# A sliding-window attention, Fourier and two-matrix kernel on one core: half of W1's casts on VectorE, fewer filler matmuls, batch 1 and a transform's column steps placed closer

## The chip, the core and the metric

The kernel runs on one core of a Trainium2 chip. The metric is the device time of one execution, in microseconds (us); the median of several runs stands for a kernel. An engine runs its own instructions in the order in which the program lists them for it, so an instruction that waits holds up all behind it on that engine.

## The reference, cut to what matters

```
# q, k, v: 8 batches, 8 heads, 576 positions, 64 wide; window 128
scores = q @ k.T / 8 + slope[h] * -(i - j)     # where 0 <= i-j < 128, else -1e9
attn   = exp(scores - max) / (sum + 1e-9)
x      = attn @ v                              # laid out as (8, 576, 512)
X      = real(fft(fft(x, axis=1), axis=2))
u      = x + X
un     = (u - mean(u)) / sqrt(var(u) + 1e-6)
out    = u + max(un @ w_ch1, 0) @ w_ch2        # 512 x 2048, 2048 x 512
```

## The kernel before, in words

The program is one list of steps, each put into a queue with a time in units of its own (a step of 1 is some five microseconds on the chip). The queue is emptied in order of these times, which is the program's order; a scheduler then fixes each engine's order from it. Who moves a step's time so moves instructions on the engines.

**Attention** works on pairs of heads; there are four pairs in each of eight batches, numbered 0 to 31. Pair `p` of batch `b` begins at `BEGIN[b] + 6 * PACE[b] * j`. `scores` (L403) multiplies queries and keys, three groups of tiles per pair and two heads each (`sp0`, `sp1`). The two heads use the upper and the lower 64 rows of the array. VectorE adds the distance bias (L417), ScalarE takes the exponential (L163 of ScalarE), TensorE turns the result (`turn`, L444), ScalarE copies it out (`pt`, L447), TensorE multiplies by the values (`values`, L461, one accumulator `pv` in one bank), and VectorE divides into the batch's tile `X` (`weigh`, L482 to L486). Batches 0 and 1 do this in f32; later batches split numbers into f16 pairs.

**The weights** W1 and W2 come as 16 chunks each (`weights`). A chunk is loaded (L196) into one of four buffers for W1 and three for W2, so chunk c waits until chunk c-4 or c-3 has been used. `rebias` (L205) casts a 16-bit half of it into a staging tile, `join` (L210, VectorE) puts the halves together, and `gram` (L218, four matmuls) adds to a sum of squares. After the sixteenth chunk a total (L148) gives one scale; then `high` (L236, ScalarE) and `low` (L239, VectorE) make the f16 pair of each of eight groups.

**The Fourier transform of batch 0** (`fourier`, b = 0) is a chain written as a list of steps, `CHAIN` = 0.15 apart: three times fold (L532 to L553, VectorE) and row matmuls (L589), with 24 matmuls on zeros (L602) behind the first two; copies out (L608); the middle (L614); column matmuls (L641) for three blocks, each with `cols_out` (L652 to L656, ScalarE) and `cols_add` (L662 to L676, VectorE); then statistics (L687), the root (L693, L694 on GpSimd), the normalised rows `un` (L702), their turn on TensorE (L711) and the split into f16 (L716, L717). With that done the first feed-forward matmuls (L816, later L830) can start. These use the scaled W1, then W2. The other seven batches have a looser chain (f16, L582, L644).

`busy` issues `SPIN` = 2 matmuls of 512 columns on a constant (L310) behind each group of scores of pairs 0 to 3; their result is never read.

VectorE's instructions of the first 25 steps are tied behind batch 0's chain: where a step of the chain was put, later VectorE work stays behind it.

Of the kernel before, what the change touches and what calls it, by code (L numbers as in the profile page):

```python
# [12 lines left out]
BF16 = mybir.dt.bfloat16  # L13
I32 = mybir.dt.int32
I16 = mybir.dt.int16
AF = mybir.ActivationFunctionType
# [30 lines left out]

LB, LC = 2, 5
DFT = 24 + LC + 0.4
PACE = (0.37, 0.7, 0.85, 0.9, 0.95, 1.0, 1.0, 1.0)  # L50
CHAIN = 0.15
STRETCH = (0.5, 0.7, 1.0, 1.15, 1.25, 1.25, 1.25, 1.25)
BEGIN = (0.0, 9.2, 26.0, 46.4, 68.0, 90.8, 114.8, 138.8)
FORWARD = (22, 41.6, 64.7, 88.7, 112.7, 136.7, 160.7, 184.7, 208.7)
SPIN = 2


def begin_of(p):
    b, j = divmod(p, 4)
    return BEGIN[b] + 6 * PACE[b] * j  # L60


def transform_of(b):
    return BEGIN[b] + PACE[b] * DFT

# [10 lines left out]
def attn_fft_ffn_kernel(  # L76
# [17 lines left out]
    V, A, G, T = nc.vector, nc.scalar, nc.gpsimd, nc.tensor  # L94
# [12 lines left out]
    rel_sb = const.tile([128, 1152], BF16, name="rel_sb")  # L107
# [38 lines left out]
    def total(m):  # L146
        sums = ps_d.tile([128, 512], F32, name="pd")[:, 0:m.shape[1]]
        T.matmul(sums, misc[:, 7:8].broadcast_to([128, 128]), m, start=True, stop=True)  # L148
        return sums

    def root_inv(dst, src):
        V.tensor_scalar(dst, src, 0.5, 2.0 ** -81, ALU.mult, ALU.max)  # L152
        V.tensor_scalar(dst.bitcast(I32), dst.bitcast(I32), 1, 0x3F800000, ALU.logical_shift_right, ALU.bitwise_and)
        V.reciprocal(dst, dst)
# [4 lines left out]
    def put(t, f, *a, **kw):  # L159
        heappush(queue, (t, next(order), lambda *a: f(*a, **kw), a))  # L160
# [12 lines left out]
    def place(b, t, f, *a, **kw):  # L173
        if b == 0:
            put(t, lambda: link(f, *a, **kw))
        else:
            put(t, lambda: f(*a, **kw))
# [5 lines left out]
    def weights(wi, t0, dt, t1, dt1):  # L183
        w, top = ((w1, 2.0 ** 7), (w2, 2.0 ** 14))[wi]
        raws, box = {}, {}
        if wi == 0:
            stages = [hbuf[:, o:o + 1024] for o in range(0, 4096, 1024)]
        else:
            third = dft.tile([128, 2, 4, 256], F16, name="uT", bufs=3).rearrange("p e c t -> p (e c t)").bitcast(F32)
            stages = [stage[:, 0:1024], stage[:, 1024:2048], third]  # L190
        ns = len(stages)

        def load(c):
            raws[c] = stages[c % ns]
            behind[0] = c if wi == 0 else -15 if c < ns else None
            nc.sync.dma_start(out=raws[c].bitcast(I16)[:, 0:2047],  # L196
                              in_=w[:, c * 512:(c + 1) * 512].bitcast(I16)[:, 1:2048])

        def words(c):
            return (wall[1][:, 0, c % 2 * 512:c % 2 * 512 + 512],  # L200
                    wall[wi][:, 1 + c // 2, c % 2 * 512:c % 2 * 512 + 512])

        def rebias(c):
            upper = words(c)[0].bitcast(F16).rearrange("p (x e) -> p x e", e=2)[:, :, 1]
            A.activation(upper, raws[c].bitcast(BF16).rearrange("p (x e) -> p x e", e=4)[:, :, 2], AF.Copy)  # L205

        def join(c):
            upper, dst = (x.bitcast(I32) for x in words(c))
            lower = raws[c].bitcast(I32).rearrange("p (x e) -> p x e", e=2)[:, :, 0]
            V.scalar_tensor_tensor(dst, lower, 13, upper, ALU.logical_shift_right, ALU.bitwise_or)  # L210

        def gram(c):
            if c == 0:
                box["gram"] = ps_f.tile([128, 512], F32, name="fp")[:, 0:128]
            upper = words(c)[1].bitcast(BF16).rearrange("p (x e) -> p x e", e=2)[:, :, 1]
            for j in range(4):
                blk = upper[:, j * 128:(j + 1) * 128]
                T.matmul(box["gram"], blk, blk, start=(c == 0 and j == 0), stop=(c == 15 and j == 3))  # L218

        def top_of():  # L220
            m1 = small.tile([128, 2], F32, name="wm1", tag="m2")
            V.tensor_reduce(m1[:, 0:1], box["gram"], AX.X, ALU.max)
            box["sums"] = total(m1[:, 0:1])

        s = wsc[:, wi:wi + 1]

        def scale():
            root_inv(s, box["sums"])
            V.tensor_scalar_mul(s, s, top * 2.0 ** -64)
            if wi == 1:  # L230
                V.tensor_tensor(wone, wsc[:, 0:1], wsc[:, 1:2], ALU.mult)
                V.tensor_scalar_mul(wone, wone, 8.0)
                V.reciprocal(wone, wone)

        def high(g):
            A.activation(wf[wi][:, g, 0], wall[wi][:, g + 1], AF.Copy, scale=s)  # L236

        def low(g):
            V.scalar_tensor_tensor(wf[wi][:, g, 1], wall[wi][:, g + 1], s, wf[wi][:, g, 0], ALU.mult, ALU.subtract)  # L239

        for c in range(16):
            t = t0 + dt * c
            put((-2.9 + 0.4 * c if wi == 0 else t0 - 1.5 + 0.1 * c) if c < ns else t + dt * (1 - ns) - 0.05, load, c)
            put(t, rebias, c)
            put(t + dt - 0.1, join, c)
            put(min(t + 3.0 * dt, t0 + 16.8 * dt) if wi == 0 else t0 + 16.5 * dt, gram, c)
        t = t0 + 17 * dt
        put(t, top_of)
        put(t + 0.3, scale)
        for g in range(8):  # L250
            put(t1 + dt1 * g, high, g)
            put(t1 + dt1 * (g + 0.8), low, g)
# [46 lines left out]
    raws, ops, Ps, pts, pvs, vmx = {}, {}, {}, {}, {}, {}  # L299
# [5 lines left out]
    spin = ps_f.tile([128, 512], F32, name="fp")  # L305
    trig = tab1_sb.rearrange("p a b c -> p (a b c)")

    def busy(p):
        for _ in range(SPIN if p < 4 else 0):
            T.matmul(spin, rel_sb[:, 0:128], rel_sb[:, 0:512], start=True, stop=True)  # L310

    def load(p):
        b, j = divmod(p, 4)
# [73 lines left out]
    def scores(p, i):  # L387
# [9 lines left out]
        for ti in grp:  # L397
            c0, m, blks = TILES[ti]
            n = 128 * len(blks)
            for x, (qq, kk) in enumerate(prods):  # L400
                for e in range(2):
                    h = slice(64 * e, 64 * e + 64)
                    T.matmul(sp[e][:m, col:col + n], qq[h, c0:c0 + m], keys(kk[h], ti),  # L403
                             start=(x == 0), stop=(x == len(prods) - 1))
            col += n
        busy(p)
        P = Ps[p, i] = {}
        for e in range(2):
# [108 lines left out]
    def fourier(b, t0):  # L517
# [201 lines left out]
        if b == 0:  # L719
            uTs[b] = []  # L720
            steps = [(begin, ), (fold_b, 2), (rows_of, (0, 1, 2), 2), (idle, 24), (fold_a, 0), (fold_b, 0), (rows_of, (0, 1, 2), 0),
                     (idle, 24), (fold_a, 1), (fold_b, 1), (rows_of, (0, 1, 2), 1)]
            for g in range(3):
                steps += [(rows_out, g)]
                if g == 0:
                    steps += [(rows_of, (3, ), c) for c in (2, 0, 1)]
            steps += [(rows_out, 3), (middle_of, ), (middle_out, ), (cols, 1), (cols_out, 1), (cols, 0), (cols_add, 1), (stats, 1), (mirrored, 1),
                      (cols_out, 0), (cols_add, 0), (stats, 0), (root, 0), (spread, 0), (spread, 1), (split, 0), (split, 1), (cols, 2), (stats, 3),
                      (mirrored, 0), (cols_out, 2), (cols_add, 2), (stats, 2), (root, 1), (spread, 2), (spread, 3)]
            last = 1 + max(i for i, (g, *a) in enumerate(steps) if g is split and a == [1])  # L730
            for i, (g, *a) in enumerate(steps):
                (place if i < last else lambda b, t, f, *a: put(t, f, *a))(b, t0 + CHAIN * i, g, *a)
            return

        f = STRETCH[b]
        place(b, t0, begin)
# [6 lines left out]
        t = t0 + f * 2.6  # L743
# [19 lines left out]
    def norm(b, of, t1):  # L763
# [15 lines left out]
        G.tensor_tensor(rstd[:, :n], rstd[:, :n], half[:, :n], ALU.pow)  # L779
        f = min(STRETCH[b], 1)  # L780
        if t1 is None:
# [58 lines left out]
    for p in range(4 * B):  # L840
        b, j = divmod(p, 4)
        t, f = begin_of(p), PACE[b]
        if b == 0:
# [10 lines left out]
        else:  # L854
            t0, late = begin_of(p - 1), 0 if p == 4 * NF else 1.3 * (p == 4 * NF + 1)
            t0 = 19.2 if p == 4 * NF else t0 - 2.9
# [24 lines left out]
    for b in range(B):  # L881
        t = begin_of(4 * b)
        fourier(b, transform_of(b))
        n = 80 if b % 2 else 64
        t = FORWARD[b]
        put(t, step, ffn(b), t, (FORWARD[b + 1] - t) / n)
# [2 lines left out]
    put(8.5, nc.sync.dma_start, out=tab2_sb, in_=tab2)  # L889
    put(8.45, nc.sync.dma_start, out=exact2, in_=tab3[:, 6 * NS:])  # L890
    weights(0, 0, 0.42, 7.6, 0.2)
    weights(1, 9.5, 0.45, 17.5, 0.12)
    traced, seen = nc.cur_bb.bb.instructions, 0
    tied = {mybir.EngineType.DVE}
    while queue:
# [6 lines left out]
        for i in fresh:  # L902
            e = i.engine
# [125 lines left out]
```

## Time and profile before

| | |
|---|---|
| median of 3 runs | 1071.96 us (1069.84 to 1074.96) |
| the profiled execution | 1071.43 us, its span 1069.6 us |
| busy, share of the span | TensorE 97%, VectorE 65%, ScalarE 52%, GpSimd 2% |
| mean granted TensorE clock | 0.991 |

The span runs from the first to the last instruction. What is read below are the views of this one execution: the page, the waits, the order of time of an engine, and tables by stretch.

### The profile page before, as it was taken

The numbers are of one execution on the slowest core, as the hardware profiler recorded it, in microseconds if no ns is written. First come the engines' busy times: TensorE is split into PE (matmuls) and PEld (weight loads), VectorE is DVE, ScalarE is ACT, GpSimd is POOL, SyncE is SP. The second block draws the span as 40 slices with busy tenths as digits, with TensorE's granted clock in tenths as the row PEclk, the third lists the DMA queues.
The fourth block names the chain that finished last, engine by engine and source line by source line (L and its number), as shares of the span: only waits on it lengthen the run. The fifth ranks groups of instructions, "written<-read, shape, count | busy, mean of one in ns | idle before, by whom it ended". The sixth has DMA issues, their size and how long they took to land.

```text
span 1069.6 us, 23236 instructions
## 1 busy us (share of the span) xinstructions
PE 1038.0 (97%) x9209; PEld 728.7 (68%) x9209; DVE 700.4 (65%) x2100; ACT 557.9 (52%) x1225; POOL 26.0 (2%) x66
## 2 busy tenths in 40 slices
PE   7997999998999999999999999998999999999998
PEld 4786785856576776766676766766677676857655
DVE  3687878687675878797776857787695835262111
ACT  6976774567544565667636645567554621241000
POOL 0000000000000000000000000000000000000000
PEclk9998899999999999999999999999999999999999
DMA  9946214337523373437333533437331420030000
GB/s 359 324 133 194 56 36 103 68 55 161 94 58 76 76 144 91 90 73 158 70 89 61 117 85 72 107 61 161 69 91 26 87 58 11 11 60 11 20 10 21
DMA packets 179789, 97.51 MB, mean 91 GB/s; under 512 B 153952, under 2 KB 162144, under 8 KB 179680
## 3 DMA queue, kind: packets, MB, share of 16 engines
q1 hardware_dynamic: 179392, 95.72, 37.5%
q8 instruction: 72, 1.18, 0.4%
q14 instruction: 37, 0.30, 0.1%
q10 hardware_dynamic: 288, 0.30, 0.1%
HBM read 49.33 MB, written 9.44 MB: 55 GB/s over the span
## 4 chain that ended last, share of the span: by engine, by line
PE 77%; DVE 11%; DMA 7%; ACT 3%; issue 2%; SPq 0%; ACTq 0%; DVEq 0%
PE fp L830 31%; PE fp L816 29%; PE sp L403 5%; DMA pt<-P 4%; PE pv L461 3%; PE pd L582 3%; DVE P L417 1%; PE sp L444 1%; DMA wall<-q_dram 1%; PE pd L644 1%; DVE P L163 1%; PE pv L467 1%; DVE hbuf L163 1%; PE pv L471 1%; PE pv L470 1%
## 5 line engine op out<-in xcount | busy, mean ns | idle before, releaser
L830 PE MATMUL fp<-wall,hbuf 128*128 128x512 f16 x1728 | 391.7, 379 | 1.7 <-DVE hbuf L163 0.9
L816 PEld LDWEIGHTS <-wall 128*128 128x128 f16 x3840 | 337.8, 98 | 55.7 <-issue 15.5
L816 PE MATMUL fp<-uT,wall 128*128 128x256 f16 x3072 | 365.2, 274 | 5.6 <-DVE hbuf L163 4.6
L830 PEld LDWEIGHTS <-hbuf 128*128 128x128 f16 x1728 | 162.7, 98 | 184.6 <-issue 3.8
L163 ACT ACTIVATE P<-P,nb 128x256 f32<-128x256 f32 x320 | 139.2, 479 | 94.4 <-DVE nb L417 93.9
L821 ACT ACTIVATE hbuf<-fp 128x512 f16<-128x512 f32 x144 | 84.9, 590 | 165.0 <-PE fp L816 164.7
L163 DVE SCALAR_TENSOR_TENSOR hbuf<-fp,hbuf 128x512 f16<-128x512 f32 x144 | 98.8, 686 | 101.0 <-ACT hbuf L821 100.5
L163 DVE SCALAR_TENSOR_TENSOR P<-P 128x384 f16<-128x384 f32 (+1 forms) x144 | 78.3, 552 | 46.6 <-ACT P L428 46.4
L417 DVE CUSTOM_DVE_ANT_0 P<-sp,rg,nsl 128x256 f32<-128x256 f32 x240 | 97.8, 450 | 13.7 <-PE sp L403 7.3
L428 ACT ACTIVATE P<-P 128x384 f16<-128x384 f32 (+1 forms) x144 | 73.1, 517 | 39.4 <-DMA pt<-P 30.0
L403 PE MATMUL sp<-kk,qq 64*128 64x256 f16 (+3 forms) x800 | 75.8, 276 | 1.0 <-ACT qq L378 0.8
L163 DVE SCALAR_TENSOR_TENSOR X<-fp,misc,X 128x512 f32<-128x512 f32 x32 | 23.8, 744 | 51.6 <-PE fp L830 51.6
L467 PE MATMUL pv<-vhs,pt 128*128 128x65 f16 x432 | 54.2, 195 | 0.8 <-DVE m L152 0.7
L470 PE MATMUL pv<-vl,pt 128*128 128x64 f16 x432 | 54.3, 193 | 0.0
L471 PE MATMUL pv<-vhs,pt 128*128 128x65 f16 x432 | 54.1, 193 | 0.0
L467 PEld LDWEIGHTS <-pt 128*128 128x128 f16 x432 | 41.0, 98 | 10.0 <-issue 1.8
L816 PE MATMUL fp<-wall,wall 128*128 128x128 f16 x768 | 45.5, 219 | 2.1 <-DVE hbuf L163 1.9
L470 PEld LDWEIGHTS <-pt 128*128 128x128 f16 x432 | 40.4, 99 | 7.8
L403 PEld LDWEIGHTS <-qq 64*128 64x128 f16 x720 | 28.9, 94 | 20.8 <-issue 14.2
L471 PEld LDWEIGHTS <-pt 128*128 128x128 f16 x432 | 40.7, 98 | 0.2
L582 PE MATMUL pd<-tab_sb,fh 128*128 128x289 f16 x168 | 37.4, 288 | 0.9 <-DVE zl L598 0.9
L417 DVE CUSTOM_DVE_ANT_0 P<-sp,rel_sb 128x256 f32<-128x256 f32 x80 | 28.4, 392 | 15.0 <-PE sp L403 14.8
(190 smaller groups left out, 1204.9 us busy)
## 6 DMA issues: line engine op xcount, KB each, us to landing
qr<-q_dram SPq DMA_DIRECT2D x28, 304.0 KB, 3.4
out_dram<-X SPq DMA_DIRECT2D x32, 256.0 KB, 2.3
hbuf<-w_dram SPq DMA_DIRECT2D x16, 511.8 KB, 7.5
vr<-v_dram SPq DMA_DIRECT2D x23, 320.0 KB, 3.1
kr<-k_dram SPq DMA_DIRECT2D x24, 289.0 KB, 3.0
X<-w_dram SPq DMA_DIRECT2D x11, 511.8 KB, 4.0
uT<-w_dram SPq DMA_DIRECT2D x5, 511.8 KB, 4.5
pt<-P SPq DMA_TRANSPOSE x144, 3.0
```

The costliest lines, as they stand in the source:

```text
L163: put(now[0] + dt, lambda: f(*a, **kw))
L403: T.matmul(sp[e][:m, col:col + n], qq[h, c0:c0 + m], keys(kk[h], ti), start=(x == 0), stop=(x == len(prods) - 1))
L417: V.tensor_tensor_reduce(pt[:m, 0:n], sp[e][:m, col:col + n], tab[:m, pc:pc + n], mul, 3.0e38, ALU.add, ALU.min, nb[:m, ti:ti + 1])
L428: A.activation(hi, P32, AF.Copy, scale=2.0 ** 14)
L461: T.matmul(pv[:, ti], pt[:, col:col + 128], ops[p][2][:, e, vc], start=first, stop=last)
L467: o = T.matmul(pv[:, ti], ph, vh[:, e, vc], start=first, stop=False)
L470: T.matmul(pv[:, ti, 0:D], ph, vl[:, e, vc], start=False, stop=False)
L471: T.matmul(pv[:, ti], pl, vh[:, e, vc], start=False, stop=last)
L582: T.matmul(zp[:, :NS], st["in", c][l][:m, g], tab1_sb[:m, (0 if g < 2 else 2) + t, c], start=(c == 0 and p == 0), stop=(c == 2 and p == 2))
L816: T.matmul(fp[:, i * n:(i + 1) * n], w1_ap(e, c, f0 + i), uT[:, j, c, 0:n], start=(c == 0 and p == 0), stop=(c == 3 and p == 2))
L821: A.activation(ht[:, 0], fp, AF.Relu)
L830: T.matmul(op, hh[f][:, a, i * 128:(i + 1) * 128], w2_ap(e, f), start=(f == 0 and p == 0), stop=(f == 15 and p == 2))
```

## The change

Six edits. (1) The casts of W1's chunks 1, 3, 5 and so on go to VectorE; the even ones and all of W2's stay on ScalarE. (2) The filler matmuls stand only behind the scores of pairs 0 and 1, and are kept where the program puts them. (3) Batch 1's pairs begin at 8.5 and are 3.6 steps apart, where they began at 9.2 and were 4.2 apart. (4) Batch 0's chain goes on at 0.08 a step from its sixteenth step. (5) W2's chunks are 0.35 of a step apart, not 0.45. (6) W2's `high` and `low` start at 16, not 17.5.

```
-PACE = (0.37, 0.7, 0.85, 0.9, 0.95, 1.0, 1.0, 1.0)
+PACE = (0.37, 0.6, 0.85, 0.9, 0.95, 1.0, 1.0, 1.0)
 CHAIN = 0.15
+DENSE = (16, 0.08)
-BEGIN = (0.0, 9.2, 26.0, 46.4, 68.0, 90.8, 114.8, 138.8)
+BEGIN = (0.0, 8.5, 26.0, 46.4, 68.0, 90.8, 114.8, 138.8)
...
-            A.activation(upper, raws[c].bitcast(BF16).rearrange("p (x e) -> p x e", e=4)[:, :, 2], AF.Copy)
+            half_of = raws[c].bitcast(BF16).rearrange("p (x e) -> p x e", e=4)[:, :, 2]
+            if wi == 0 and c % 2:
+                V.tensor_copy(upper, half_of)
+            else:
+                A.activation(upper, half_of, AF.Copy)
...
     def busy(p):
-        for _ in range(SPIN if p < 4 else 0):
-            T.matmul(spin, rel_sb[:, 0:128], rel_sb[:, 0:512], start=True, stop=True)
+        for _ in range(SPIN if p < 2 else 0):
+            tc.keep_in_program_order(T.matmul(spin, rel_sb[:, 0:128], rel_sb[:, 0:512], start=True, stop=True))
...
-                (place if i < last else lambda b, t, f, *a: put(t, f, *a))(b, t0 + CHAIN * i, g, *a)
+                (place if i < last else lambda b, t, f, *a: put(t, f, *a))(b, t0 + (CHAIN * i if i < DENSE[0] else CHAIN * DENSE[0] + DENSE[1] * (i - DENSE[0])), g, *a)
...
     weights(0, 0, 0.42, 7.6, 0.2)
-    weights(1, 9.5, 0.45, 17.5, 0.12)
+    weights(1, 9.5, 0.35, 16, 0.12)
```

The changed file has five more lines, so its lines stand up to five further down: L210 before is L215, L417 is L422, L711 is L716.

What this does to the engines' orders is shown at three places. The first is VectorE's order near the program's start, from the join of W1's second chunk to the first scores of pair 1 (`sp0_243`). Before:

```order
L210 SCALAR_TENSOR_TENSOR wall0_103<-hbuf_102,wall1_104 128x512 x2
L417 ISA P_204,nb_203<-sp0_197,rel_sb_90 128x256
L417 ISA nb_203 128x1
L417 ISA P_207,nb_206<-sp1_198,rel_sb_90 128x256
L417 ISA nb_206 128x1
L210 SCALAR_TENSOR_TENSOR wall0_103<-hbuf_102,wall1_104 128x512 x2
L417 ISA P_252,nb_251<-sp0_243,rel_sb_90 128x256
```

And in the changed kernel:

```order
L208 CAST wall1_104<-hbuf_102 128x512
L215 SCALAR_TENSOR_TENSOR wall0_103<-hbuf_102,wall1_104 128x512
L422 ISA P_204,nb_203<-sp0_197,rel_sb_90 128x256
L422 ISA nb_203 128x1
L422 ISA P_207,nb_206<-sp1_198,rel_sb_90 128x256
L422 ISA nb_206 128x1
L215 SCALAR_TENSOR_TENSOR wall0_103<-hbuf_102,wall1_104 128x512
L422 ISA P_252,nb_251<-sp0_243,rel_sb_90 128x256
```

Before, pair 1's first scores stand behind the joins of chunks 1, 2, 3 and 4; now behind a cast and the joins of chunks 1 and 2 alone.

The second place is VectorE's order at the end of batch 0's chain, from the column block that is added second (`ab_1063` before, `ab_1087` now) to the rows that TensorE turns (`un`). Before:

```order
L210 SCALAR_TENSOR_TENSOR wall1_104<-uT_109,wall1_104 128x512
L662 TENSOR_TENSOR ds_1087<-ab_1063 128x257
L663 TENSOR_TENSOR ds_1087<-ab_1063 128x256
L485 RECIPROCAL ri_1059<-ri_1059 128x5
L665 TENSOR_TENSOR X_311<-X_311,ds_1087 128x512
L486 TENSOR_TENSOR X_1058<-pv_961,ri_1059 128x5x64
L687 BN_STATS st_1103<-X_311 128x6
L688 BN_AGGR ag_1050<-st_1103 128x2
L693 TENSOR_SCALAR rstd_1051<-ag_1050 128x2
L210 SCALAR_TENSOR_TENSOR wall1_104<-X_107,wall1_104 128x512
L702 TENSOR_SCALAR un_1116<-X_311,ag_1050,rstd_1051 128x512
```

And in the changed kernel:

```order
L667 TENSOR_TENSOR ds_1100<-ab_1087 128x257
L668 TENSOR_TENSOR ds_1100<-ab_1087 128x256
L670 TENSOR_TENSOR X_311<-X_311,ds_1100 128x512
L692 BN_STATS st_1104<-X_311 128x6
L693 BN_AGGR ag_1078<-st_1104 128x2
L215 SCALAR_TENSOR_TENSOR wall1_104<-X_107,wall1_104 128x512
L698 TENSOR_SCALAR rstd_1079<-ag_1078 128x2
L707 TENSOR_SCALAR un_1115<-X_311,ag_1078,rstd_1079 128x512
```

The division of batch 1's values (L485, L486) has gone ahead of the chain's end, and the last join now stands ahead of the root's first step, where it stood behind it; it is the join of W2's chunk 13 (chunks counted from 0), before it was that of chunk 12.

The third place is TensorE's order at the same spot, from the last column matmul to the turn of `un`. Before (L218 are W2's sums of squares, four for each chunk):

```order
L641 MATMUL pd_1146<-hbuf_102 33x127
L218 LDWEIGHTS wall1_104
...
L218 MATMUL fp_1207<-wall1_104 128x128
L461 MATMUL pv_1109<-vr_688,pt_862 128x65 x3
L461 MATMUL pv_1109<-vr_688,pt_954 128x65 x4
L461 MATMUL pv_1109<-vr_688,pt_1041 128x65 x2
L218 LDWEIGHTS wall1_104
...
L218 MATMUL fp_1207<-wall1_104 128x128
L711 MATMUL sp0_1118<-ident_85,un_1116 128x128 x4
```

And in the changed kernel:

```order
L646 MATMUL pd_1154<-hbuf_102,zr_973 33x128 x2
L646 MATMUL pd_1154<-hbuf_102 33x127
L466 MATMUL pv_1064<-vr_640,pt_797 128x65 x3
L466 MATMUL pv_1064<-vr_640,pt_894 128x65 x4
L466 MATMUL pv_1064<-vr_640,pt_984 128x65 x2
L223 LDWEIGHTS wall1_104
L223 MATMUL fp_1195<-wall1_104 128x128
...
L716 MATMUL sp0_1117<-ident_85,un_1115 128x128 x4
```

The values have moved ahead of the sums of squares. Of these, 48 matmuls (chunks 0 to 11) stood ahead of the values and 4 (chunk 12) behind them; now all 56 of chunks 0 to 13 stand in one block behind the values.

## Rows read from the trace of the kernel before

**Rows 1.** The page, part 1 and 2: busy, and the clock by slices.
```profile
PE 1038.0 (97%) x9209; PEld 728.7 (68%) x9209; DVE 700.4 (65%) x2100; ACT 557.9 (52%) x1225; POOL 26.0 (2%) x66
...
PEclk9998899999999999999999999999999999999999
```

**Rows 2.** TensorE's waits, to 125 us, then behind: total, times, longest.
```profile
PE sp L403 <- DMA wall<-k_dram: 5.1, 1, 5.1
PE fp L218 <- DVE wall L210: 4.6, 3, 2.9
...
PE fp L816 <- DVE hbuf L163: 6.6, 7, 1.8
...
PE pv L467 <- DVE m L152: 0.7, 2, 0.5
```

**Rows 3.** TensorE in order of time, to 68 us: start, length, idle before.
```profile
8.43 3.97 PE L310 MATMUL fp<-rel_sb 128*128 128x512 bf16 x14
...
13.21 0.70 PE L403 MATMUL sp<-wall,qq 64*128 64x256 f32 x4
...
14.09 2.32 PE L310 MATMUL fp<-rel_sb 128*128 128x512 bf16 x10
17.05 1.09 PE L444 MATMUL sp<-ident,P 128*128 128x128 f32 x8 [0.64 <-ACT pt L447]
...
21.17 0.41 PE L218 MATMUL fp<-wall 128*128 128x128 bf16 x4 [1.33 <-DVE wall L210]
...
38.88 0.70 PE L403 MATMUL sp<-wall,qq 64*128 64x256 f32 x2
...
65.44 2.12 PE L461 MATMUL pv<-wall,pt 128*128 128x65 f32 x18
```

**Rows 4.** ScalarE, then VectorE, in order of time near the start.
```profile
15.89 0.78 ACT L205 ACTIVATE wall<-hbuf 128x512 f16<-128x512 bf16 x1 [2.82 <-DMA hbuf<-w_dram]
...
16.70 0.69 DVE L210 SCALAR_TENSOR_TENSOR wall<-hbuf,wall 128x512 int32<-128x512 int32 x1 [2.91 <-ACT wall L205]
...
22.63 0.42 DVE L417 CUSTOM_DVE_ANT_0 P<-sp,rel_sb 128x256 f32<-128x256 f32 x1
```

**Rows 5.** VectorE in order of time through batch 0's chain.
```profile
71.70 0.68 DVE L532 TENSOR_TENSOR fg<-X 128x512 f32<-128x512 f32 x1
...
82.93 0.76 DVE L553 TENSOR_TENSOR hbuf<-pm 128x256 f32<-128x256 f32 x2
...
84.30 1.28 DVE L239 SCALAR_TENSOR_TENSOR wall<-wall,misc 128x1024 f16<-128x1024 f32 x1
...
93.00 0.43 DVE L662 TENSOR_TENSOR ds<-ab 128x257 f32<-128x257 f32 x1 [3.23 <-ACT ab L656]
...
102.56 1.00 DVE L702 TENSOR_SCALAR un<-X,ag,rstd 128x512 f32<-128x512 f32 x2 [0.60 <-POOL rstd L694]
```

**Rows 6.** TensorE in order of time at the chain's end, and at 255 us.
```profile
98.59 0.48 PE L218 MATMUL fp<-wall 128*128 128x128 bf16 x4 [2.89 <-DVE wall L210]
100.39 4.10 PE L461 MATMUL pv<-vr,pt 128*128 128x65 f32 x18 [1.31 <-DVE X L486]
...
104.72 1.06 PE L711 MATMUL sp<-ident,un 128*128 128x128 f32 x4
...
109.69 0.42 PE L816 MATMUL fp<-uT,wall 128*128 128x256 f16 x1
...
255.13 4.45 PE L816 MATMUL fp<-uT,wall 128*128 128x256 f16 x24 [1.84 <-DVE hbuf L163]
```

**Rows 7.** Stretches: length; busy of PE, PEld, DVE, ACT, POOL; granted clock; DMA.
```profile
98.78:112.43 13.65, 12.34 (x56) 9.73 (x54) 9.05 (x23) 6.93 (x16) 1.18 (x2) 0.50 0.36 104
255.79:259.20 3.41, 3.41 (x19) 2.41 (x17) 2.92 (x9) 3.09 (x9) 0.00 (x0) 0.50 0.30 61
98.78:104.72 5.94, 4.63 (x26) 4.37 (x24) 4.12 (x11) 2.39 (x7) 1.18 (x2) 0.50 0.56 166
```

**Rows 8.** DMA issues: count, size, median us to landing.
```profile
X<-w_dram SPq DMA_DIRECT2D x11, 511.8 KB, 4.0
```

## The prediction

> **What bounds the kernel now.** The page first: TensorE is busy for 97% of the span, VectorE for 65%, ScalarE for 52% [rows 1]. So what counts is time that TensorE waits, time that it spends on work nobody needs, and time at the lower clock. The clock line of the page has its low digits in the first eighth of the span alone; there I looked closer. TensorE's waits up to 125 us come to 12.9 us, of which 5.1 are the first load, which no edit touches, and 4.6 are three waits of a sum of squares (L218) for a join (L210) on VectorE [rows 2]. The three stand in TensorE's order of time: 1.33 at 21.17 and 0.39 at 27.28 [rows 3], and 2.89 at 98.59, which is followed by 1.31 for `X` [rows 6]. Behind 125 us eight kinds of wait come to 14.0 us, the largest 6.6 [rows 2]. The stretches then say what the clock costs: from 98.78 to 112.43 TensorE is granted 0.50, its lower level of 1.2 GHz, and is busy 12.34 of 13.65 us, so half of it, 6.2 us, is lost; of this 4.63 busy us, 2.3 lost, lie before L711 at 104.72. From 255.79 to 259.20 it falls once more, and 1.7 us are lost [rows 7]. Each time TensorE had just been idle: 2.89 us with four matmuls before 98.78, 1.84 us at 255.13; the first fall ended 2.7 us behind the first feed-forward matmul at 109.69 [rows 6].
>
> **The change part by part.** I follow the program in four stretches, and ask of each how much earlier its last step comes.
>
> *Fillers.* L310 is there 24 times: 14 from 8.43 for 3.97 us and 10 from 14.09 for 2.32 us [rows 3], 0.26 each with the overlap taken off. Twelve stay, behind the six groups of pairs 0 and 1; twelve go, 12 x 0.26 = 3.1 us. What did the fillers cover? Behind the first lot the exponentials that the transposes need were ready, so that lot delayed work. The second lot lay over a wait: ScalarE's cast of chunk 2 begins at 15.89, after 2.82 us without data [rows 4], and the transposes at 17.05 waited 0.64 even behind the fillers [rows 3]. So some of the 3.1 us could come back as a wait. I count the full 3.1 here and put the waits into the next term, which is the one that holds the chunks.
>
> *The front's order.* Before, VectorE takes pair 1's first scores at 22.63, behind the joins of chunks 1 to 4; now they stand behind the join of chunk 2, which is done by 17.4 [rows 4]. TensorE is thus fed about 5 us sooner. Of its 0.64 + 1.33 + 0.39 = 2.36 us of idle here [rows 3] I expect about 1.3 to stay, because the sum of squares of chunk 2 is still ahead of the scores and cannot start before 17.3: gain 1.0. The bounds: all 2.36 gained, or 3 lost, when a filler's cover is missing for as long as the second lot lasted (2.32) and the 0.64 is repeated.
>
> *Pairs that stand side by side.* Two heads' scores use different rows of the array. At 13.21 four records (two matmuls of 256, one of each head) take 0.70 us as listed, and at 38.88 two records (one matmul alone) take 0.70 too [rows 3]; so the second head is free where its matmul stands next to the first one's. In the changed order four groups of pairs 2 to 4 come to stand in this way, and one of pair 1 no longer does: net three more, at half of a pair's time each. I take 0.45 each, -1.4 us; bounds 0 and -2.1 (3 x 0.70).
>
> *W1's odd casts on VectorE.* Eight, of a form that the trace of before has not on this engine. The nearest row is a join of the same 128x512, 0.69 us [rows 4]; the lower bound is `un`, 0.50 each [rows 5]. So 4 to 5.5 us more on VectorE, spread over 30 us in which it has idle time of 0.9 us and more in front of joins (2.91 at 16.70 [rows 4]); ScalarE loses 8 x 0.78. What hides it is this idle time. If it were gone, 5 us would fall on TensorE through the scores' bias on the same engine. I count 0.
>
> Front: -3.1 - 1.0 - 1.4 = **-5.5 us** at the end of pair 3's values, before at 65.44 + 2.12 = 67.56 [rows 3], now near 62.
>
> *The chain.* From the first fold (L532, 71.70) to the end of the third fold (82.93 + 0.76 = 83.69 [rows 5]) VectorE now has one `low` (L239) more, because W2's part begins at 16 and not 17.5, one join more, and two more scores of batch 1, which is closer. By rows: 1.28 for L239 [rows 5], 0.69 for a join and 2 x 0.42 for scores [rows 4], less 0.3 of overlap, 2.5; and 0.5 for a wait for ScalarE's `high`: **+3.0** (bounds +2.5 and +5). Up to the second block's `cols_add` (93.00) the same work remains in the same order, 9.3 us: 0. From there to `un` it took 10.1 us (to the first of two at 102.56 [rows 5]). Four scores, the division and one join have left this piece: 1.3 + 0.4 + 0.6 = 2.3 less, 7.8. Then, before, TensorE was not free for L711 until 104.72, 1.7 us after `un` was there, since its values ran for 4.10 us at half clock [rows 6]; now the values stand ahead of the sums of squares. So -2.3 - 1.7 = -4.0, and with 0.4 us for the place of the first fold and the handover: 0.2 + 3.0 - 4.0 + 0.2 = **-0.6** (bounds -3 and +5). The upper bound is the last join: it is now that of W2's chunk 13 and stands ahead of the root on VectorE. A load of a chunk takes 4.0 us to land [rows 8] and waits for the buffer that the join of chunk 10 frees; every us that it is late, the statistics' root, `un`, L711 and all feed-forward work behind it are late too.
>
> So L711 comes at 104.72 - 5.5 - 0.6 = **98.6**. Three of the transposes and a chunk's four sums of squares that stood behind L711 or just ahead of it are done before: -0.5.
>
> *The clock.* The sums of squares of W2 are now one block of 56 behind the values. 48 can run (44 took 2.68 us [rows 6]); then TensorE waits for two joins and for `un`, some 5 us in all, from about 93 to 98.6. By the row at 98.59 such idle time brings the clock down. I expect the fall shortly before L711 and the rise again 2.7 us behind the first feed-forward matmul, near 109: 11 busy us at half, 5.5 lost behind L711. Before, behind L711 it was (12.34 - 4.63) / 2 = 3.85 [rows 7]. So **+1.6**.
>
> *Behind 112 us.* The last 5,103 of some 8,900 matmuls stand in the same sequence in both. Between lies a stretch in which a batch-1 transform block has changed places with a feed-forward block; the idle time of 14.0 us [rows 2] and the fall at 255.79 [rows 7] lie partly there. I know no sign: 0, bounds -3 and +4.
>
> **Sum:** -5.5 - 0.6 - 0.5 + 1.6 = -5.0 on the profiled 1071.4 (span 1069.6 and 1.8 around it, 0.5 below the median): **1066.5**, which is 0.5% less. About 0.5%, 5.4 us, is also what a measurement of this kernel can tell from no change.
>
> **The rivals.**
> *The clock holds at the chain's end* (B). If the joins of chunks 12 and 13 come early, because chunks are 0.35 apart and not 0.45, TensorE has no long gap ahead of L711. Then the 5.5 us are not lost: 1061. For it: ScalarE has 6 us less to do. Against: chunk loads go by buffers, not by their times.
> *The lead is lost on VectorE* (C). The front ends 5 us sooner, yet the chain is VectorE's from 71.70 to 83.69, without idle time [rows 5], and it got `low`, joins and scores on top. With the upper bound of the chain the sum is -5.5 + 5 + 1.6 - 0.5: 1072. For it: the late join ahead of the root.
> *The clock falls in the front* (D, slower). The fillers of pairs 2 and 3 are what ran while chunk 2 was awaited. Without them TensorE is idle about where the 0.64 and the 1.33 stood, and what follows are short f32 pieces. If the clock then falls, every busy us costs 0.5 more. To end over 0.5% slower, at 1077.4, it must lose 10.9 us against my sum, so 22 us at half clock: a fall at 17 that lasts to 39. For it: 1.84 us brought it down at 255 [rows 6], and from 98.78 on it stayed down for 13.65 us in which TensorE was busy for 90% [rows 7]. Against: 1.33 us of idle at 21.17 brought no fall [rows 1, 3], and pairs follow closely from 28 on. Time 1077 to 1082. The Trainium skill, "TensorE: Matmul & The Clock Gate", in "HAM oscillation — how this bites in real kernels", says that bursts of matmuls with waits between them lose the full clock, and pay for each burst; by that rule the front is at risk. The trace agrees at 98.78 and 255.79 and not at 21.17.
> *New stalls behind 112 us* (E), at the upper bound of that term or somewhat above: 1070 to 1078.
>
> **How the numbers follow.** My forecast has 0.42, with a range of its own of 1064 to 1069.5; since it lies near the bound of 1066.6, 0.25 of it is faster and 0.17 the same. B 0.17, faster. C 0.16, the same. D 0.12, slower. E 0.13, of which 0.10 the same and 0.03 slower. Faster 0.25 + 0.17 = 0.42; same 0.17 + 0.16 + 0.10 = 0.43; slower 0.15. The range goes from 1059.5, a little below B, to 1074, and leaves out D, the worst of E and a little of B, 0.19.
>
> **What would show it.** L310 twelve times; pair 3's values done near 62 (62 to 64.5 if idle time takes the fillers' place); the first fold near 66.6, the third done near 81.5 (over 83 is C); L711 near 98.6; 0.50 granted from about 97 to 109, and nowhere before 90 (a fall there is D, none at 97 is B); TensorE's waits behind 125 us still near 14. Wrong above all if W2's chunks 12 and 13 are joined at another time than I think, since the gap, the clock and the root all hang on them.

## The result, and the profile after

The changed kernel takes 1061.78 us (median of 4 runs, 1061.08 to 1063.18), the kernel before beside it 1073.01: a ratio of 0.9905, 95% interval 0.9887 to 0.9923. The forecast was 1066.5, range 1059.5 to 1074. The profiled execution has a span of 1060.2 us against 1069.6, so 9.4 us have gone; the forecast had 5.0. Some executions of a kernel take 20 us or more longer than its others, at a lower granted clock: the ratios below go by the others, and since the profile of the kernel e2 is of such an execution, its cells in the table below stay empty.

The page of the changed kernel, busy times and clock by slices:

```profile
PE 1032.3 (97%) x9197; PEld 723.1 (68%) x9197; DVE 703.7 (66%) x2108; ACT 554.0 (52%) x1217; POOL 25.5 (2%) x66
...
PEclk9998999999999999999999999999999999999999
```

TensorE's busy time is 5.7 us less than in [rows 1], its idle time 3.7 us less (31.6 to 27.9), and the low digit is still there. TensorE's waits, up to 125 us and behind (total, times, longest):

```profile
PE fp L223 <- DVE wall L215: 6.0, 4, 2.9
...
PE fp L821 <- DVE hbuf L164: 4.4, 8, 1.3
```

Against [rows 2] the joins are waited for longer (4.6 to 6.0), and the feed-forward matmuls' largest wait for VectorE has shrunk from 6.6 to 4.4; all waits behind 125 us come to 10.3, 14.0 before. TensorE in order of time in the front (start, length, idle before):

```profile
8.57 1.80 PE L315 MATMUL fp<-rel_sb 128*128 128x512 bf16 x4
...
14.21 0.40 PE L223 MATMUL fp<-wall 128*128 128x128 bf16 x4 [0.74 <-DVE wall L215]
...
18.26 0.41 PE L223 MATMUL fp<-wall 128*128 128x128 bf16 x4 [0.75 <-DVE wall L215]
...
41.64 0.41 PE L223 MATMUL fp<-wall 128*128 128x128 bf16 x4 [1.60 <-DVE wall L215]
...
59.09 2.12 PE L466 MATMUL pv<-wall,pt 128*128 128x65 f32 x18
```

The fillers come in fours and twos behind their scores, where [rows 3] has 14 and 10 in a lump; pair 3's values end at 61.21, not 67.56. The next is VectorE, an odd chunk's cast near the start and then the chain's marks:

```profile
12.96 0.46 DVE L208 CAST wall<-hbuf 128x512 f16<-128x512 bf16 x1 [0.78 <-DMA hbuf<-w_dram]
...
65.52 0.68 DVE L537 TENSOR_TENSOR fg<-X 128x512 f32<-128x512 f32 x1
...
80.54 0.42 DVE L558 TENSOR_TENSOR hbuf<-pm 128x256 f32<-128x256 f32 x1
...
88.93 0.43 DVE L667 TENSOR_TENSOR ds<-ab 128x257 f32<-128x257 f32 x1 [0.51 <-ACT ab L661]
...
95.03 0.66 DVE L215 SCALAR_TENSOR_TENSOR wall<-X,wall 128x512 int32<-128x512 int32 x1
95.61 0.16 DVE L698 TENSOR_SCALAR rstd<-ag 128x2 f32<-128x2 f32 x1
96.60 1.00 DVE L707 TENSOR_SCALAR un<-X,ag,rstd 128x512 f32<-128x512 f32 x2 [0.83 <-POOL rstd L699]
```

From the first fold to the third it takes 15.4 us (65.52 to 80.96), 12.0 in [rows 5]. TensorE at the chain's end:

```profile
89.68 3.15 PE L223 MATMUL fp<-wall 128*128 128x128 bf16 x52
95.75 0.61 PE L223 MATMUL fp<-wall 128*128 128x128 bf16 x4 [2.92 <-DVE wall L215]
97.20 1.12 PE L716 MATMUL sp<-ident,un 128*128 128x128 f32 x4 [0.84 <-DVE un L707]
...
104.21 0.40 PE L821 MATMUL fp<-uT,wall 128*128 128x256 f16 x1
```

L716 starts at 97.20, where [rows 6] has L711 at 104.72. The stretches (length; busy of PE, PEld, DVE, ACT, POOL; granted clock; DMA) of the changed kernel, the last one from L716 to the end:

```profile
95.48:109.13 13.65, 12.54 (x46) 8.51 (x47) 10.09 (x28) 8.02 (x20) 0.71 (x1) 0.50 0.15 44
97.20:109.13 11.93, 11.93 (x42) 8.16 (x43) 9.20 (x25) 6.86 (x15) 0.00 (x0) 0.50 0.17 51
607.48:610.89 3.41, 3.41 (x15) 1.45 (x14) 3.38 (x17) 1.01 (x2) 0.00 (x0) 0.50 0.83 183
97.20:1060.19 962.99, 948.61 (x8557) 657.26 (x8557) 631.92 (x1882) 480.77 (x1055) 20.66 (x47) 0.99 0.34 73
```

And of the kernel before, from L711 to the end:

```profile
104.72:1069.65 964.93, 946.42 (x8566) 657.05 (x8564) 632.13 (x1882) 480.49 (x1059) 19.68 (x47) 0.99 0.34 73
```

The clock still falls at the chain's end, for 13.65 us as before, now with 11.93 busy us of it behind L716 (7.71 before, [rows 7]). The short fall has gone from 255 us to 607 us. Idle time behind L711 or L716, length less busy, is 18.5 us before and 14.4 now.

So the 9.4 us are: 6.4 at pair 3's values, 1.2 more by L716, 1.9 behind it; in that, 4.1 less idle time stand against 2.1 more at half clock.

What the scores cost TensorE can be read from the same view for their line alone, up to the end of pair 3's values; before, now:

```profile
5.14:67.56 62.42, 23.45 (x99) 14.32 (x99) 1.00 0.86 310
```

```profile
5.28:61.21 55.93, 19.28 (x98) 11.25 (x98) 1.00 0.93 345
```

The same scores keep TensorE busy 4.2 us less. Pair 2's first group shows how: its two heads stood apart before, each taking as long as both take together now.

```profile
28.26 0.92 PE L403 MATMUL sp<-wall,qq 64*128 64x256 f32 x4
...
31.71 0.92 PE L403 MATMUL sp<-wall,qq 64*128 64x256 f32 x4
```

```profile
28.07 0.92 PE L408 MATMUL sp<-wall,qq 64*128 64x256 f32 x8
```

In TensorE's order of time, five of the twelve groups of pairs 0 to 3 have their two heads side by side before and eight now (five gained, two lost). The fillers' line in these stretches fell from 6.29 to 4.22, and the idle time rose from 2.5 to 3.4.

### The profile page after: what moved, and what is told of

Same layout as the page of the kernel before. It is cut to its first block, busy times and chain, and to the rows that moved or that the text cites. A ratio compares the mean times of both kernels' runs of the same rounds, so it can differ in the third digit from the quotient of the medians.

```text
span 1060.2 us, 23194 instructions
## 1 busy us (share of the span) xinstructions
PE 1032.3 (97%) x9197; PEld 723.1 (68%) x9197; DVE 703.7 (66%) x2108; ACT 554.0 (52%) x1217; POOL 25.5 (2%) x66
## 4 chain that ended last, share of the span: by engine, by line
PE 78%; DVE 9%; DMA 7%; ACT 4%; issue 2%; SPq 0%; POOL 0%; ACTq 0%; DVEq 0%
PE fp L835 31%; PE fp L821 31%; PE sp L408 5%; DMA hbuf<-w_dram 3%; PE pd L587 3%; DMA pt<-P 3%; PE pv L466 2%; PE pd L649 1%; DVE P L422 1%; PE pv L472 1%; PE pv L476 1%; PE sp L449 1%; PE pv L475 1%; DVE hbuf L164 1%; DVE P L164 1%
## 5 line engine op out<-in xcount | busy, mean ns | idle before, releaser
L422 DVE CUSTOM_DVE_ANT_0 P<-sp,rg,nsl 128x256 f32<-128x256 f32 x240 | 97.9, 453 | 24.5 <-PE sp L408 19.6
L408 PE MATMUL sp<-kk,qq 64*128 64x256 f16 (+3 forms) x800 | 78.0, 278 | 1.0 <-ACT qq L383 1.0
L408 PEld LDWEIGHTS <-qq 64*128 64x128 f16 x720 | 30.0, 94 | 22.9 <-issue 16.9
L570 ACT ACTIVATE fh<-abcd,sc 128x512 f16<-128x512 f32 (+1 forms) x21 | 15.1, 720 | 41.7 <-DVE abcd L558 38.4
```

The lines of the kernel that those rows point to most:

```text
L422: V.tensor_tensor_reduce(pt[:m, 0:n], sp[e][:m, col:col + n], tab[:m, pc:pc + n], mul, 3.0e38, ALU.add, ALU.min, nb[:m, ti:ti + 1])
```

## The experiments

Twelve kernels, each run beside the kernel before; ratios are to it. In the table "scores" is the scores' busy time up to the end of pair 3's values, "half" is half of TensorE's busy time in the stretches granted 0.50, and "idle" is TensorE's idle time behind L711 (its line in that kernel); these are from one execution each, which lies up to 3.4 us from the median of its kernel.

| kernel | ratio, 95% interval | scores | values end | L711 | half | idle | span |
|---|---|---|---|---|---|---|---|
| before | 1 | 23.5 | 67.56 | 104.72 | 7.9 | 18.5 | 1069.6 |
| changed | 0.9905, 0.9887 to 0.9923 | 19.3 | 61.21 | 97.20 | 8.0 | 14.4 | 1060.2 |
| e1 fillers alone | 0.9931, 0.9910 to 0.9952 | 17.0 | 58.75 | 98.50 | 6.2 | 18.5 | 1061.8 |
| e9 24 kept in place | 0.9978, 0.9963 to 0.9992 | 18.3 | 61.33 | 102.96 | 12.7 | 19.6 | 1070.5 |
| e10 12 free | 0.9968, 0.9957 to 0.9980 | 22.0 | 65.51 | 105.26 | 6.4 | 18.8 | 1067.9 |
| e11 fillers, closer steps | 0.9934, 0.9918 to 0.9950 | | 59.85 | 94.55 | 8.0 | 18.3 | 1063.2 |
| e2 fillers back | 0.9953, 0.9927 to 0.9978 | | | | | | |
| e5 casts back | 0.9901, 0.9878 to 0.9924 | | 61.42 | 97.86 | 6.4 | 15.3 | 1057.6 |
| e6 batch 1 back | 0.9952, 0.9931 to 0.9974 | | 58.89 | 96.67 | 10.1 | 19.3 | 1067.1 |
| e7 steps back | 0.9984, 0.9965 to 1.0004 | | 60.93 | 102.72 | 11.8 | 19.7 | 1070.6 |
| e8 W2 back | 0.9905, 0.9876 to 0.9935 | | 60.75 | 94.87 | 10.2 | 17.9 | 1061.2 |
| e3 gap filled, 15 | 0.9876, 0.9847 to 0.9905 | | 59.98 | 96.12 | 0.0 | 16.7 | 1054.7 |
| e4 gap filled, 16 | 0.9890, 0.9860 to 0.9920 | | 60.81 | 97.09 | 1.7 | 17.2 | 1056.3 |
| e12 W2 back, gap filled | 0.9838, 0.9820 to 0.9856 | | 61.41 | 95.56 | 1.7 | 16.9 | 1051.7 |

Of the 0.95% by which the changed kernel is shorter, the fillers' edit alone gives 0.69% (e1). What the other five edits add to it is not clear of the noise, since the two intervals overlap.

**The fillers' edit alone (e1).** On the kernel before:

```
-        for _ in range(SPIN if p < 4 else 0):
-            T.matmul(spin, ...)
+        for _ in range(SPIN if p < 2 else 0):
+            tc.keep_in_program_order(T.matmul(spin, ...))
```

> The kernel before with the fillers' edit alone (12 instead of 24 matmuls of L310, kept in the program's place). Theory 1, the fillers are work ahead of the scores and transposes and cost what they last: 12 x 0.26 = 3.1 us earlier at pair 3's values (before 67.56), of which 0 to 2.3 come back as waits near 14 to 18 us; the whole kernel 1 to 3 us shorter than the kernel before. Theory 2, they cover a wait: values end where they did, within 0.5 us, and the time is the same. Theory 3, the clock falls in the front without them: 0.50 granted somewhere between 14 and 40 us, and the kernel is 2 us or more longer.

Values came 8.8 us sooner, far over theory 1's 3.1, and the clock did not fall in the front. The scores' line of e1, up to the end of pair 3's values:

```profile
5.47:58.75 53.28, 17.00 (x97) 10.49 (x97) 1.00 0.97 360
```

6.5 us of the 8.8 are in the scores' busy time; the fillers' own time is the smaller part. That asks which half of the edit does it.

**Kept but 24 (e9), fewer but free (e10).** Each is one half of that edit, on the kernel before (`p < 4` kept in place; `p < 2` left to the scheduler).

> The kernel before with all 24 fillers, but each kept where the program puts it (the second half of the fillers' edit alone). Theory P, the place counts: kept fillers close each group of scores, so the two heads' matmuls stand side by side (16 instead of 9 in pairs 0 to 3 by the order), scores up to pair 3's values take about 17 us instead of 22.3, the values end near 62 instead of 67.56 (58.75 with 12 kept), and the kernel is 4 to 6 us shorter than the one before. Theory N, the number counts: scores' time stays, the values end within 1 us of before and so does the end.

> The kernel before with 12 fillers that the scheduler may move (the first half of the fillers' edit alone). Theory P (place): the two heads' scores stand apart as before (the order has 8 side by side in pairs 0 to 3, before 9), scores take about 22 us; only the fillers' own time is saved, values 2.5 to 3 us sooner than 67.56 and the kernel 1 to 3 us shorter than before. Theory N (number): values near 59 as with 12 kept, and the kernel 6 us or more shorter.

The scores' line of e9, then of e10, and TensorE in e10 near the start:

```profile
5.20:61.33 56.13, 18.26 (x98) 11.41 (x98) 1.00 0.93 344
```

```profile
5.64:65.51 59.87, 22.03 (x97) 13.56 (x97) 0.97 0.88 321
```

```profile
8.94 3.94 PE L310 MATMUL fp<-rel_sb 128*128 128x512 bf16 x12
...
17.80 0.78 PE L444 MATMUL sp<-ident,P 128*128 128x128 f32 x4 [2.83 <-ACT pt L447]
```

For the front theory P holds: keeping the place is worth 6.2 us at the values (5.2 in the scores), fewer fillers 2.1. Where 12 stand free in one lump, the wait that the second lump covered appears, 2.83 us at 17.80, and the clock falls for 3.41 us at 18.19. For the whole kernel P missed: e9 gains 0.2%, not 4 to 6 us. Its lead is 1.8 us at L711, and 12.7 us are lost at half clock, which falls at 67, 98, 251 and 726 us in its profile.

**The fillers back (e2).** The changed kernel with the two lines of before.

> The changed kernel with the 24 fillers of before (pairs 0 to 3, where the scheduler puts them). Theory 1 (cost what they last): pair 3's values end 3.1 us later than in the changed kernel (61.21), near 64.3, and the end comes 2 to 3 us later, 1064 to 1065. Theory 2 (they only cover waits): values within 0.5 us of 61.21, end within 1 us of 1061.8. The order of TensorE behind L716 is that of the changed kernel, so waits behind 125 us should stay at about 10 us by both.

It has no profile that can be read beside the others. The ratio lies 0.005, about 5 us, above that of the changed kernel; the intervals allow 0.4 to 10 us, so theory 1 fits, and theory 2 hardly.

**The casts back (e5), W2 back (e8).**

```
-            if wi == 0 and c % 2:
+            if wi == 2:
```
```
-    weights(1, 9.5, 0.35, 16, 0.12)
+    weights(1, 9.5, 0.45, 17.5, 0.12)
```

> The changed kernel with all of W1's casts on ScalarE again. Theory 1 (hidden, the prediction's 0): the time stays within 1 us of the changed kernel, since the eight casts lie in idle time of either engine. Theory 2: VectorE is the engine that feeds TensorE in the front, so that giving the casts back ends pair 3's values 1 to 3 us sooner than 61.21, and the kernel as much. Theory 3: ScalarE is that engine, and the values and the end come 2 us or more later.

> The changed kernel with W2's chunks 0.45 apart and its high and low from 17.5 as before. Theory 1 (the prediction's +3.0): the chain from the first to the third fold has one low less on VectorE and is 2 to 3 us shorter than in the changed kernel (65.52 to 80.9), but the last join is later by as much; L716 within 1 us of 97.20 and the end within 1.5 us of the changed kernel. Theory 2: the closer chunks shorten the wait for the last join, so L716 comes 2 us or more later than 97.20 and the end too. Theory 3: the low's earlier place is a pure loss, and this kernel ends 2 us or more sooner than the changed one.

Neither changes the time beyond its interval: theory 1 for e5, and for e8 theory 1 as to the time. A cast on VectorE takes 0.46 us; what moving eight of them costs is too small for the ratios, which leave some 3 us open either way. With W2 back the first to the third fold takes 13.6 us, not 15.4, and L716 comes 2.3 us sooner, which no theory had; the end does not, since 2.2 us more are lost at half clock and idle time behind L716 is 3.5 us more.

**Batch 1 back (e6), the steps back (e7).**

```
-PACE = (0.37, 0.6, ...    BEGIN = (0.0, 8.5, ...
+PACE = (0.37, 0.7, ...    BEGIN = (0.0, 9.2, ...
```
```
-DENSE = (16, 0.08)
+DENSE = (16, 0.15)
```

> The changed kernel with batch 1's pairs at 9.2 and 4.2 apart as before. Theory 1 (the prediction's chain): two scores of batch 1 fewer on VectorE in the chain, L716 0 to 1 us sooner than in the changed kernel (97.20); but the sequence of TensorE from 115 to 500 us is about that of before, so the waits behind 125 us come to 13 us or more and the end is 1 to 3 us later, 1063 to 1065. Theory 2, batch 1's place is what gives the gain behind the chain: the end comes 4 us or more later. Theory 3, it does nothing: within 1 us of the changed kernel.

> The changed kernel with the chain's steps 0.15 apart throughout. Theory 1: the closer steps let the chain pass scores, the division and a join on VectorE (2.3 us by the prediction), so without them the second block's addition to L716 takes 2 us or more longer than the 8.3 us of the changed kernel, and the end is 2 to 4 us later, 1064 to 1066. Theory 2: the order at the chain's end is set by what is ready, not by the steps' times: L716 within 0.5 us of 97.20 and the end within 1 us, but for what the sequence behind 115 us, which is here that of before, costs (0 to 3 us).

The waits of TensorE from 200 to 300 us in e6, and the stretch of e7 behind its fall:

```profile
PE fp L821 <- DVE hbuf L164: 3.9, 4, 2.8
```

```profile
102.35:122.83 20.48, 20.48 (x75) 14.30 (x75) 15.17 (x45) 9.61 (x21) 0.00 (x0) 0.50 0.00 1
```

Both are worth more than either theory 1 said. With batch 1 back (5 us longer than the changed kernel by the ratios) the values and L716 come sooner, and it is lost behind: idle time of 19.3 us, of it a wait of 2.8 us at 251.57 that the changed kernel has not; e6 answers to theory 2. With the steps back the kernel is the one before in time, 0.9984: L716 at 102.72, 5.5 us later (theory 1), a fall of 20.48 us instead of 13.65, and 5.3 us more idle time behind, which theory 1 had not priced. Most of the 5.5 us lies where no theory looked: from the third fold's end to the first block added it takes 11.8 us (80.63 to 92.40), 8.0 in the changed kernel; from there to L716 it takes 10.3, not 8.3.

**Fillers and closer steps alone (e11).** The two edits on the kernel before.

> The kernel before with two of the six edits: 12 kept fillers, and the chain's steps 0.08 apart from the sixteenth. Theory 1, these two carry the gain and the other four cost or give nothing: values near 58.75 as with the fillers alone, L711 (98.50 there) 3 to 5 us sooner, and the kernel 1059 to 1063. Theory 2, the closer steps only mend what W2's earlier chunks and the closer batch 1 do to the chain: L711 within 1 us of 98.50 and the kernel within 1.5 us of the fillers alone (0.993 of before).

L711 comes 4.0 us sooner than in e1, as theory 1 says, and the time is that of e1, as theory 2 says. From L711 to the end, e1 and e11:

```profile
98.50:1061.79 963.29, 944.84 (x8566) 656.24 (x8564) 632.56 (x1882) 480.26 (x1059) 19.77 (x47) 1.00 0.35 74
```

```profile
94.55:1063.21 968.66, 950.32 (x8601) 660.70 (x8601) 636.36 (x1896) 483.27 (x1066) 19.72 (x47) 0.99 0.35 75
```

Behind L711 stand 35 matmuls more: work of batch 1 and sums of squares that filled the chain now follow it. Of the 5.5 us that TensorE is busy longer there, 2.9 are lost at half clock (6.7 in all, 3.7 in e1), and 2.5 are this work. Idle time there is the same, 18.3 against 18.5. So here, moving the chain ahead of other work of an engine that is full anyway gives nothing; in the changed kernel the same steps are worth 8.5 us by the ratios (e7), with less idle time and less half clock.

**The gap filled (e3, e4, e12).** On the changed kernel, fillers into a free part of the bank of the sums of squares; e4 with 4 instead of 3, e12 with `{9: 16, 10: 3}` and W2 as before:

```
                 T.matmul(box["gram"], blk, blk, ...)
+            for _ in range({12: 12, 13: 3}.get(c, 0) if wi else 0):
+                tc.keep_in_program_order(T.matmul(box["all"][:, 128:512],
+                    rel_sb[:, 0:128], rel_sb[:, 0:384], start=False, stop=False))
```

> The changed kernel with 15 filler matmuls of 384 columns in the gap at the end of batch 0's chain, 12 between the sums of squares of W2's chunks 12 and 13 and 3 behind those of chunk 13 (not read; nothing else moves in TensorE's order). In the changed kernel TensorE idles 2.92 us there, and 0.50 is granted from 95.48 for 13.65 us. Theory A, the idle time alone brings the clock down: with the gap filled it stays at 1.00, the 11.8 busy us behind L716 take about 5.9 less, and the kernel ends near 1056. Theory B, the kind of work around it (narrow f32 matmuls, waits for VectorE) brings it down: the fall is there anyway, the end within 1 us of 1061.8. Between them: a fall that comes later and lasts less long.

> As the run before, with 16 fillers, 4 behind the sums of squares of chunk 13. The one filler more (0.2 us) makes the scheduler give TensorE, from some 115 us to some 500 us, about the sequence that the kernel before has, where the run with 15 keeps that of the changed kernel. So the pair tells what the sequence behind the chain is worth. Theory C, the 3.7 us that the changed kernel gains behind 125 us (waits 14.0 before, 10.3 now) come from this sequence: this run ends 2 to 4 us later than the one with 15, and its waits behind 125 us come to about 13 to 14 us. Theory D, they come from the earlier end of batch 0's chain: both end within 1 us of each other.

> The changed kernel with W2's chunks and its high and low at the times of before, and 19 filler matmuls of 384 columns in the gap at the chain's end (16 between the sums of squares of chunks 9 and 10, where it waits 3.32 us, 3 behind them). By theory A (the idle time brings the clock down) 0.50 is not granted there, L716 stays near 94.9, and the 5 us of clock and some of the 1.7 of a second short fall at 122 are saved: 1054 to 1057, the shortest of all. By theory B the fall is there and the end is 1060 to 1062.

TensorE in e3 at the chain's end, and the stretch in which the changed kernel was at 0.50:

```profile
91.32 2.11 PE L226 MATMUL fp<-rel_sb 128*128 128x384 bf16 x12
94.66 0.41 PE L224 MATMUL fp<-wall 128*128 128x128 bf16 x4 [1.23 <-DVE wall L215]
94.91 0.65 PE L226 MATMUL fp<-rel_sb 128*128 128x384 bf16 x3
96.12 0.66 PE L719 MATMUL sp<-ident,un 128*128 128x128 f32 x4 [0.56 <-DVE un L710]
```

```profile
95.48:109.13 13.65, 13.09 (x85) 9.23 (x84) 12.32 (x38) 10.22 (x28) 0.00 (x0) 1.00 0.17 46
```

The clock stays up, and the four transposes of `un` take 0.66, not 1.12. Here theory A holds: the wait brings it down, not the narrow f32 work, which is the same. All executions agree with it: the mean granted clock of five of e3's six is 0.996 to 1.000 (0.992 in the sixth), and 0.992 to 0.994 in the changed kernel's four. But a fall needs no wait. In e8, TensorE was busy without a break for 8 us before one:

```profile
114.37:122.37 8.00, 8.00 (x58) 6.22 (x56) 6.41 (x27) 2.54 (x7) 0.69 (x1) 1.00 0.19 40
122.37:125.78 3.41, 3.41 (x19) 2.73 (x17) 1.71 (x14) 2.99 (x8) 0.00 (x0) 0.50 0.81 101
```

Of the 8.0 us that e3's profile saves (6.3 of them here, 1.7 at 607 us), 2.3 come back as idle time behind the chain (16.7 against 14.4), so the end is 5.5 us sooner in the profile; by the ratios it is 3 us, with intervals that overlap. By the traces, e4 has the matmuls in the order of before from 267 us on (the changed kernel and e3 only from 484 and 479): 1.5 us later than e3 in the medians, with intervals that overlap, idle time 0.5 more and a short fall at 714 (1.7). What the order is worth stays open; theory C's 2 to 4 us are not shown. e12, TensorE at the chain's end:

```profile
90.90 2.76 PE L226 MATMUL fp<-rel_sb 128*128 128x384 bf16 x16
94.42 0.40 PE L224 MATMUL fp<-wall 128*128 128x128 bf16 x4 [0.76 <-DVE wall L215]
94.66 0.65 PE L226 MATMUL fp<-rel_sb 128*128 128x384 bf16 x3
95.56 0.66 PE L719 MATMUL sp<-ident,un 128*128 128x128 f32 x4 [0.26 <-DVE un L710]
```

It has W2's old times and a filled gap, no fall here (one of 3.41 us stands at 37), and is the shortest, 1055.64 us: 0.9838 of before.

## Why the prediction was right, step by step

The direction and the range held, and of its cases the forecast, not a rival, describes the profile. In size it had luck: 1061.8 us lies outside the forecast's own range (1064 to 1069.5), and within the whole range because that reaches down to rival B; and the sign was hardly called, with 0.42 for faster and 0.43 for the same. The profiled time lies 4.4 us under the forecast, nearly all of it by the last term.

*The front*, -5.5 forecast, -6.4 measured: the sum came near by luck, with the parts mis-sized. Pairs side by side: -1.4 forecast, -4.2 measured. The net count of three groups held in pairs 0 to 3; its price did not. The step took 0.45 us for each; the group at 28.07 gains 0.92, and a lost group of one tile costs 0.7 (0.70 at 13.21 in [rows 3], now 1.38 at 11.55). e9 and e10 show which half of the edit does it: the fixed place of the fillers is what closes each group of scores (e9 against before -5.2, e10 against before -1.4). The Trainium skill, "TensorEngine Tiling (Array Packing)", section "When to Use Tiling", gives 2x row tiling for a contraction of 64 rows; the trace agrees where the two heads stand next to each other in TensorE's order (0.92 us for both at 28.07), and not where they stand apart (0.92 us for each). Fillers: -3.1 forecast, -2.1 measured, as the twelve that stay take 4.22, 0.35 each and not 0.26. The feeding order, -1.0 forecast: idle time rose by 0.9 instead; waits of 0.74, 0.75 and 1.60 for joins are there. These come to -5.4; the other 1.0 lies in the other lines (the values keep TensorE busy 0.9 less) and was not followed. The casts: 0 forecast, and e5 finds no difference.

*The chain*, -0.6 forecast, -1.2 measured, its pieces close: first to third fold +3.0, measured 3.4 (e8: 1.8 of it W2's earlier `high` and `low`); up to the first block added (93.00 before, which the prediction calls the second block's) 0 forecast, -1.3 measured; from there to L711 -4.0 forecast, -3.4 measured. The closer steps make most of that last gain (11.7 us without them in e1, 8.0 in e11; 10.3 in e7, 8.3 in the changed kernel), and without them the piece that the prediction put at 0 is 3.8 us longer (e7).

*The clock*, +1.6 forecast, measured (11.93 - 7.71) / 2 = 2.1. The fall came at 95.48, not 97, and lasted to 109.13, as said. By the Trainium skill's "HAM oscillation — how this bites in real kernels" ("TensorE: Matmul & The Clock Gate"), which the forecast had beside rival D, waits between bursts cost the clock; e3 bears it out, 0.50 to 1.00 with the wait filled. That rule of the Trainium skill does not cover the fall of e8 at 122.37, which no wait precedes. Rival B (the clock holds) has its time, not its cause: TensorE still waited 2.92 us for a join, and the fall is there. Rival C did not happen: the third fold ends at 80.96, where C has over 83. Nor did D: no stretch below 1.00 before 95 us; nor E: idle time behind the chain fell.

*Work done ahead*, -0.5 forecast: 0. Busy time behind L711 less the half-clock loss is 946.42 - 3.86 - 1.71 = 940.85 before and 948.61 - 5.97 - 1.71 = 940.93 now.

*Behind 112 us*, 0 forecast with bounds -3 and +4: the step that failed in size. Idle time there went from 18.5 to 14.4, -4.1, below its bound. Over the kernels of the table that goes with two edits together: 18.3 to 19.7 us wherever batch 1 is at its old place or the steps are 0.15 apart (before, e1, e6, e7, e9, e10, e11), 14.4 to 17.9 where both are new. The cause stays open. It is not the order alone: in the last 5,117 matmuls, which stand in the same order in both, TensorE idles 11.2 us before (from 492.89 on) and 9.1 now (from 484.31), and three kernels with the same 7,127 matmuls at the end idle 12.8 (before, from 280.89), 11.9 (e4) and 15.0 (e7) there. With one execution of each kernel, part of the 4.1 us may be what executions differ by; e3 and e4 do not separate it.

## What to carry to other kernels

Filler work that a scheduler may move is not neutral even where it is short: where it stands decides which real matmuls come to stand side by side, and here that was worth more than the fillers' own time at the end of pair 3's values, though of e9's 6.2 us there only 0.2% of the whole time was left at the end. On an engine that is full, a chain that ends sooner helps only by the idle time and the half-clock time that go with it; look at both behind the chain, and not at the chain's end alone. A known wait that brings the clock down can be filled on purpose: 19 small matmuls are all that e12's program has more than e8's, and 7 us lie between the two by the ratios, with intervals that do not overlap.

## What the runs showed of the hardware

Two heads' scores of 64 rows each take TensorE 0.92 us together when they stand side by side in its order (the changed kernel, 28.07), and 0.92 us each when other matmuls stand between them (before, 28.26 and 31.71).

No length of idle time by itself goes with a fall of the clock. It fell behind idle times of 1.84 (before, at 255 us) and 2.83 us (e10), and behind none in e8 at 122.37. It did not fall in e3 behind 1.23 us with 0.56 close by, nor behind 2.70 (e1, at 247.87) and 3.09 us (e10, at 255.01). How long it stayed low differed as much: 3.41 us in e10, where TensorE was then busy without a break, and 13.65 us in the changed kernel and 20.48 in e7, where it was also busy without a break behind L716. What brings it back is not shown.
